# Strips of a Toeplitz convolution: half-strips on two queues, two channel pairs of prefetch, and a fourth strip

## Chip, cores, metric

The kernel runs on one core of a Trainium2 chip (trn2). The metric is the device time of one execution in microseconds (us). Each kernel was run four times, the kernel before up to seven times beside it. The kernel before takes 2420 us.

## The reference

Two stages follow one another. The first is a causal long convolution along the sequence, per channel; the second is a token mixer with two large dense matrices.

```python
B, S, D = 8, 5696, 128
def _attn_ref(x, h):                      # x: B,S,D   h: S,D
    L = 2 * S
    Yf = np.fft.rfft(x, n=L, axis=1) * np.fft.rfft(h, n=L, axis=0)[None]
    return np.fft.irfft(Yf, n=L, axis=1)[:, :S, :].astype(np.float32)
def _moe_ref(x, w_theta, w_tok_r, w_tok_i, w_ch):
    theta = x @ w_theta
    y = einsum('ts,bsd->btd', w_tok_r, x * cos(theta)) + einsum('ts,bsd->btd', w_tok_i, x * sin(theta))
    u = x + y
    return u + np.maximum(u @ w_ch, 0.0)
```

Only the convolution matters here; it is done in bf16 by matrix products instead of an FFT.

## The kernel before

The sequence is cut into 45 blocks of 128. For each channel `d` and each lag `k` of 0 to 44, TensorE multiplies a 128x128 Toeplitz block of `h` with the blocks of `x` that lag so far behind. A Toeplitz block is a window of a "strip": partition `p` of a strip holds the padded filter row of the channel, shifted by `p` elements, so the load is a DMA whose source rows start 2 bytes apart. The lags are cut into strips. Two of them are loaded into 64 partitions only, with 64 extra columns; the other 64 partitions are the same data shifted by 64 and are copied on the chip. The third is loaded in full.

```python
LAGS = ((0, 2 * KX, 64), (2 * KX, 31, 64), (31, NT, 0))      # KX = 8, NT = 45
# pool of strips: bufs=4 for each of strip0, strip1, strip2, stripq
def conv_strips(d):
    for n_, (k0, k1, halo) in enumerate(LAGS):
        w = (k1 - k0) * P
        strip = csb.tile([P, w + halo], BF16, ...)
        if halo == 0:                       # all 128 partitions
            nc.sync.dma_start(strip, AP(h_pad, [[1, P], [1, w]]));  continue
        lower = (d + n_) % 2 == 0
        own, other, c0, c1 = (lower half, upper half, 0, 64) if lower else (upper, lower, 64, 0)
        nc.sync.dma_start(strip[own, :], AP(h_pad, [[1, 64], [1, w + 64]]))
        if n_ == 0: nc.vector.tensor_copy(strip[other, c0:c0 + w], strip[own, c1:c1 + w])
        else:       nc.scalar.activation(strip[other, c0:c0 + w], strip[own, c1:c1 + w], AF.Copy)
    q_ = stripq;  nc.vector.tensor_add(q_, s0_[:, c0:c0 + w], s0_[:, c0 + P:c0 + P + w])
def conv_prepare(d):                        # a pair of channels
    xp = ...;  nc.scalar.activation(xp, xy[:, :, :, d:d + 2], AF.Copy)
    strips = [conv_strips(d + e) for e in range(2)]
    vd = ...;  nc.vector.tensor_sub(vd, xp even blocks, xp odd blocks)

nxt = conv_prepare(0)
for d in range(0, D, 2):
    xp, vd, strips = nxt
    nxt = conv_prepare(d + 2)               # one pair ahead, as written
    for e in range(2):
        # ... 8 products into c_ps, 17 of strip0 and stripq, 29 of the other strips into r_ps
    nc.scalar.activation(c_sb, c_ps, AF.Copy)
    nc.vector.tensor_tensor(xy even, r_ps even, c_sb, op=add)        # and odd: subtract
```

The code is shortened; `...` stands for what was left out. `stripq` holds sums of neighbouring blocks of `strip0`, and `vd` differences of neighbouring blocks of `x`; they spare products and stay as they are.

In the timelines shown below, ScalarE runs its instructions in the order in which they were built into the program. "Order" below always means that of the built program.

Of the kernel before, what the change touches and what calls it, by code (L numbers as in the profile page):

```python
# [11 lines left out]
BF16 = mybir.dt.bfloat16  # L12
add = mybir.AluOpType.add
mult = mybir.AluOpType.mult
AF = mybir.ActivationFunctionType
# [6 lines left out]
def kernel(  # L22
# [10 lines left out]
    nc = tc.nc  # L33
    B, S, D = x.shape
    assert D == 128
    P = 128
    NT = (S + P - 1) // P
    Sp = NT * P
    S_last = S - (NT - 1) * P
    HW = Sp + P  # L40
# [11 lines left out]
    h_pad = h_pad_h.ap()  # L52
# [25 lines left out]
    with tc.tile_pool(name="s0", bufs=1) as s0, \  # L78
# [27 lines left out]
        for tj in range(NT):  # L106
            q_cnt = P if tj < NT - 1 else S_last
            tmp = xl.tile([P, B, D], F32, tag="xt")
            if q_cnt < P:
# [3 lines left out]
                                      ap=[[D, q_cnt], [S * D, B], [1, D]]))  # L113
# [15 lines left out]
    KX = 8  # L129
    NJ2 = (NT + 1) // 2  # L130
    assert NT == 2 * NJ2 - 1
    LAGS = ((0, 2 * KX, 64), (2 * KX, 31, 64), (31, NT, 0))
    with tc.tile_pool(name="conv_strip", bufs=4) as csb, \
         tc.tile_pool(name="conv_x", bufs=3) as cxb, \
         tc.tile_pool(name="conv_psum", bufs=2, space=bass.MemoryType.PSUM) as cps:

        def conv_strips(d):

            out_ = []
            for n_, (k0, k1, halo) in enumerate(LAGS):  # L140
                w = (k1 - k0) * P
                strip = csb.tile([P, w + halo], BF16, tag=f"strip{n_}", name=f"strip{n_}")
                src = h_pad.offset + d * HW + P * k0
                if halo == 0:
                    nc.sync.dma_start(strip, bass.AP(tensor=h_pad.tensor, offset=src,
                                                     ap=[[1, P], [1, w]]))
                    out_.append((strip, 0, k0))
                    continue
                lower = (d + n_) % 2 == 0
                own, other, c0, c1 = ((slice(0, 64), slice(64, P), 0, 64) if lower else  # L150
                                      (slice(64, P), slice(0, 64), 64, 0))
                nc.sync.dma_start(strip[own, :],
                                  bass.AP(tensor=h_pad.tensor, offset=src,
                                          ap=[[1, 64], [1, w + 64]]))
                if n_ == 0:
                    nc.vector.tensor_copy(strip[other, c0:c0 + w], strip[own, c1:c1 + w])  # L156
                else:
                    nc.scalar.activation(strip[other, c0:c0 + w], strip[own, c1:c1 + w], AF.Copy)  # L158
                out_.append((strip, c0, k0))
            s0_, c0, _ = out_[0]  # L160
            w = (2 * KX - 1) * P
            q_ = csb.tile([P, w], BF16, tag="stripq", name="stripq")
            nc.vector.tensor_add(q_, s0_[:, c0:c0 + w], s0_[:, c0 + P:c0 + P + w])  # L163
            return out_, q_

        def conv_prepare(d):

            if d >= D:
                return None
            xp = cxb.tile([P, NJ2, 2, B, 2], BF16, tag="xp", name="xp")  # L170
            nc.scalar.activation(xp.rearrange("q j p b e -> q (j p b) e"),  # L171
                                 xy[:, :, :, d:d + 2].rearrange("q t b e -> q (t b) e"), AF.Copy)
            strips = [conv_strips(d + e) for e in range(2)]
            vd = cxb.tile([P, NJ2, B, 2], BF16, tag="vd", name="vd")
            nc.vector.tensor_sub(vd.rearrange("q j b e -> q j (b e)"),
                                 xp[:, :, 0, :, :].rearrange("q j b e -> q j (b e)"),
                                 xp[:, :, 1, :, :].rearrange("q j b e -> q j (b e)"))
            return xp, vd, strips

        nxt = conv_prepare(0)  # L180
        for d in range(0, D, 2):
            xp, vd, strips = nxt
            nxt = conv_prepare(d + 2)
            r_ps = cps.tile([P, 2, 512], F32, tag="rps", name="r_ps")
            c_ps = cps.tile([P, 2, 256], F32, tag="cps", name="c_ps")
            for e in range(2):
                (s0_, s1_, s2_), q_ = strips[e]
                r = r_ps[:, e, :NT * B]
                rj = r_ps[:, e, :2 * NJ2 * B].rearrange("q (j p b) -> q j p b", p=2, b=B)
                c_ = c_ps[:, e, :NJ2 * B]  # L190
                xt = xp.rearrange("q j p b e -> q (j p b) e")
                strip, c0, _ = s0_
                for k in range(KX):
                    n = NJ2 - k
                    b_ = strip[:, c0 + 2 * k * P:c0 + (2 * k + 1) * P]
                    nc.tensor.matmul(c_[:, B * k:], b_, vd[:, :n, :, e],  # L196
                                     start=(k == 0), stop=(k == KX - 1))
                    nc.tensor.matmul(rj[:, k:NJ2 - 1, 1, :], q_[:, 2 * k * P:(2 * k + 1) * P],  # L198
                                     xp[:, :n - 1, 0, :, e], start=(k == 0), stop=False)
                    nc.tensor.matmul(rj[:, k:, 0, :],  # L200
                                     q_[:, (2 * k - 1) * P:2 * k * P] if k else b_,
                                     xp[:, :n, 1, :, e], start=False, stop=False)
                nc.tensor.matmul(rj[:, KX:, 0, :], strip[:, c0 + (2 * KX - 1) * P:c0 + 2 * KX * P],
                                 xp[:, :NJ2 - KX, 1, :, e], start=False, stop=False)
                for strip, c0, k0 in (s1_, s2_):
                    k1 = LAGS[1][1] if strip is s1_[0] else NT
                    for k in range(k0, k1):
                        c = c0 + (k - k0) * P
                        nc.tensor.matmul(r[:, B * k:B * NT], strip[:, c:c + P],  # L209
                                         xt[:, :B * (NT - k), e], start=False, stop=(k == NT - 1))  # L210
            rv = r_ps[:, :, :2 * NJ2 * B].rearrange("q e (j p b) -> q p j b e", p=2, b=B)
            c_sb = cxb.tile([P, NJ2, B, 2], F32, tag="csb", name="c_sb")
            nc.scalar.activation(c_sb.rearrange("q j b e -> q (j b) e"),
                                 c_ps[:, :, :NJ2 * B].rearrange("q e n -> q n e"), AF.Copy)
            cv = c_sb
            yv = xy[:, :, :, d:d + 2].rearrange("q (j p) b e -> q p j b e", p=2)
            nc.vector.tensor_tensor(yv[:, 0], rv[:, 0], cv, op=add)  # L217
            nc.vector.tensor_tensor(yv[:, 1, :NJ2 - 1], rv[:, 1, :NJ2 - 1], cv[:, :NJ2 - 1],
                                    op=ALU.subtract)
# [147 lines left out]
    with tc.tile_pool(name="bpool", bufs=1, reuse_waits="tile") as bp, \  # L367
# [174 lines left out]
        def prepare(i, at_once=True):  # L542
            if i >= len(stretches):
                return None
            k, p, tt, j0, s0, nj = stretches[i]
            if s0 == 0:
                loads(k + 1)
            if tt is None:
                a1, a2 = (w_t(wb, s0, nj, ng=2) for wb in loaded[k])
                return a1, a2, w_sum(a1, a2, add, nj, m=64)  # L550
            w11, w22, w12, w21 = loaded[k]
            a = {}

            def step(n):

                if n == 0:
                    a[M3] = w_t(w11, s0, nj)
                elif n == 1:
                    a[M4] = w_t(w22, s0, nj)
                elif n == 2:  # L560
                    a["12"] = w_t(w12, s0, nj)
                    a[M5] = w_sum(a[M3], a["12"], add, nj)
                elif n == 3:
                    a["21"] = w_t(w21, s0, nj)
                    a[M2] = w_sum(a["21"], a[M4], add, nj)
                elif n == 4:
                    a[M1] = w_sum(a[M3], a[M4], add, nj)
                elif n == 5:
                    a[M7] = w_sum(a["12"], a[M4], ALU.subtract, nj)
                else:  # L570
                    a[M6] = w_sum(a["21"], a[M3], ALU.subtract, nj)
            if at_once:
                for n in range(7):
                    step(n)
                return a
            return a, step

        nxt, second, st = None, None, {}
        loads(0)
        for i, (k, p, tt, j0, s0, nj) in enumerate(stretches):  # L580
            first_of_pair = j0 + s0 == 0
            end_of_pair = j0 + s0 + nj == NJ
            if first_of_pair and tt == 0:
                start_pass(p)
                if p == 0:
# [4 lines left out]
                    nxt = prepare(0)  # L590
# [7 lines left out]
            a, nxt = nxt, prepare(i + 1, not woven)  # L598
            if woven:
                nxt, step = nxt  # L600
            if tt is None:
# [6 lines left out]
                for j in range(nj):  # L608
                    jj = j0 + s0 + j
                    for r in range(2):  # L610
                        b = [x[:, r, :] for x in bts[jj]]
# [7 lines left out]
                if end_of_pair:  # L619
# [5 lines left out]
                    for h in range(2):  # L625
                        c, c0 = cs[h]
# [22 lines left out]
            for n, q in enumerate(ORDER):  # L649
# [16 lines left out]
                if n == 1 and spread and (p == 1 or not end_of_pair):  # L666
                    where_bg["tags"] = ("c2", "c3") if j0 + s0 == TJ else ("red", "mag")
                    _, first, second = spread.pop(0)
# [45 lines left out]
```

## Time and profile before

Four runs took 2416.59 to 2425.41 us, median 2419.45 us. The convolution runs from about 111 us (first product) to 660 us (last), 64 pairs at about 8.6 us. What comes after it, about 1765 us, is untouched by the change.

| 200 to 500 us of the kernel before | value |
|---|---|
| TensorE busy | 251 of 300 us |
| VectorE, ScalarE busy | 171 us, 176 us |
| share of time in which the 16 DMA engines are busy | 1.04 (packets overlap a little) |
| DMA rate | 235 GB/s |

The table of windows, kernel before. The columns are the stretch and its length, then the busy time of TensorE (PE), its weight loads (PEld), VectorE (DVE), ScalarE (ACT) and GpSimd (POOL), the granted clock, the DMA share and GB/s:

```profile
core 0: us, PE busy (x) PEld busy (x) DVE busy (x) ACT busy (x) POOL busy (x), PEclk, DMA share, GB/s
200.00:500.00 300.00, 251.13 (x3830) 237.40 (x3827) 170.88 (x247) 175.72 (x142) 0.00 (x0) 0.99 1.04 235
```

The view of waits in that stretch, longest first, and below it that of the sync queue (SPq), kernel before. "DVE strip <- DMA strip<-h_pad: 113.9, 68" says that VectorE, about to copy a strip, waited 113.9 us in 68 waits for a strip to land:

```profile
DVE strip L156 <- DMA strip<-h_pad: 113.9, 68, 4.0
ACT strip L158 <- DMA strip<-h_pad: 66.2, 39, 3.0
ACT xp L171 <- PE r_ps L209: 55.1, 35, 2.3
```

```profile
SPq L152 <- DMA strip<-h_pad: 149.2, 137, 2.8
SPq L145 <- DMA strip<-h_pad: 41.1, 70, 1.3
```

The DMA issues of the strips (count, size of one, median us from issue to landing) and the chain of waits by line between 300 and 320 us, kernel before:

```profile
strip<-h_pad SPq DMA_DIRECT2D x128, 448.0 KB, 11.5
strip<-h_pad SPq DMA_DIRECT2D x128, 264.0 KB, 11.4
...
strip<-h_pad SPq DMA_DIRECT2D x128, 248.0 KB, 10.7
```

```profile
by line: DMA strip<-h_pad 104.3%; issue 9.3%; ACT strip L158 7.7%; ACT xp L171 4.9%; PE r_ps L209 3.8%; ACT c_sb L213 1.5%; ACTq L158 0.1%; ACTq L171 0.1%
```

These lines say that the copies wait for strips, that the queue itself waits for older strips to land, and that the DMA engines never rest. One transfer lands 11 us after its issue although there are six in every 8.6 us. The chain is the DMA. (A piece of the chain counts in full where it began before the stretch, so the shares can add up to more than 100%.)

### The profile page before, as it was taken

Reading aid. Unit: us, or ns where it says so; the run is one execution under the profiler, and the core shown is the slowest. Engines: PE = TensorE matmul, PEld = TensorE weight load, DVE = VectorE, ACT = ScalarE, POOL = GpSimd, SP = SyncE. Lnnn points to the kernel's source line nnn. Section 1 sums busy time; section 2 is a strip of 40 time slices with the busy share of each in tenths; the row PEclk is TensorE's granted clock in tenths of the full one; section 3 lists DMA queues with packets and bytes.
Section 4 is the critical chain, followed back from the end, with each engine's and each line's share of the span. In section 5 each row is a group of like instructions: output and inputs, shape, how many; then the busy total and the mean of one; then the engine's idle time right before and its main releaser. Section 6 shows DMA issues by size and latency. Waiting matters only on the chain.

```text
span 2426.1 us, 42014 instructions
## 1 busy us (share of the span) xinstructions
PE 2167.8 (89%) x15665; PEld 1237.5 (51%) x15838; DVE 1684.1 (69%) x3062; ACT 728.1 (30%) x861; POOL 796.7 (33%) x1474
## 2 busy tenths in 40 slices
PE   4578888888865799999999999979999999999997
PEld 1177787877742344444444444424444444444443
DVE  3355555555577788888688777787776777777774
ACT  3555655565583333333233000001110111111111
POOL 0000000000011344544445655335445445444540
PEclk8599999999997899999999999989999999999998
DMA  9999999999899789988889998878779779778872
GB/s 242 242 214 225 237 240 234 237 238 235 207 285 305 150 159 168 164 159 165 137 158 167 158 159 139 228 153 144 135 136 158 133 130 160 137 134 149 143 133 60
DMA packets 443532, 433.97 MB, mean 179 GB/s; under 512 B 66496, under 2 KB 370624, under 8 KB 443200
## 3 DMA queue, kind: packets, MB, share of 16 engines
q1 hardware_dynamic: 217488, 288.86, 45.8%
q0 software_dynamic: 222816, 131.33, 41.6%
q10 hardware_dynamic: 3024, 11.08, 1.2%
q8 instruction: 125, 2.05, 0.4%
q14 instruction: 79, 0.65, 0.1%
HBM read 477.58 MB, written 84.75 MB: 232 GB/s over the span
## 4 chain that ended last, share of the span: by engine, by line
PE 61%; DMA 24%; DVE 8%; issue 2%; ACT 2%; POOL 2%; SPq 1%; DVEq 0%; ACTq 0%; another core or an unknown queue 0%; POOLq 0%
PE m L653 50%; DMA strip<-h_pad 15%; PE r_ps L209 2%; DVE c L660 2%; DMA wb<-in_moe_w_tok_i_dram 2%; DMA tmp<-in_x_dram 2%; POOL wb L381 1%; DMA b<-zi_hbm 1%; DMA wb<-in_moe_w_tok_r_dram 1%; DMA h_bf<-in_h_dram 1%; DVE stripq L163 1%; PE r_ps L198 1%; PE utp L467 1%; PE v L474 1%; DVE wt L390 1%
## 5 line engine op out<-in xcount | busy, mean ns | idle before, releaser
L381 POOL DMA_DIRECT2D wb<-in_moe_w_tok_i_dram x720 | 389.1, 548 | 797.5 <-DVE wt L390 711.9
L381 POOL DMA_DIRECT2D wb<-in_moe_w_tok_r_dram x720 | 387.9, 548 | 777.5 <-DVE xy L217 656.6
L653 PE MATMUL m<-b,wt 128*128 128x512 bf16 x1892 | 452.7, 383 | 18.7 <-DVE b L322 6.8
L390 DVE STREAM_TRANSPOSE wt<-wb 128x384 f32<-128x384 f32 (+2 forms) x720 | 359.4, 523 | 118.3 <-PE m L653 72.4
L653 PEld LDWEIGHTS <-wt 128*128 128x128 bf16 x1936 | 190.4, 99 | 250.8 <-issue 23.2
L660 DVE TENSOR_TENSOR c<-c,m 128x512 f32<-128x512 f32 x440 | 283.3, 669 | 0.0
L158 ACT ACTIVATE strip<-strip 64x1920 bf16<-64x1920 bf16 x128 | 230.7, 1802 | 133.4 <-DMA strip<-h_pad 129.7
L469 ACT ACTIVATE uts<-utp 128x512 bf16<-128x512 bf16 (+1 forms) x90 | 53.3, 592 | 616.3 <-PE utp L467 616.3
L156 DVE COPY strip<-strip 64x2048 bf16<-64x2048 bf16 x128 | 88.2, 689 | 214.3 <-DMA strip<-h_pad 214.1
L209 PE MATMUL r_ps<-xp,strip 128*128 128x232 bf16 (+28 forms) x3712 | 228.9, 216 | 1.4 <-ACT strip L158 1.1
L198 PE MATMUL r_ps<-xp,stripq 128*128 128x176 bf16 (+7 forms) x1024 | 153.9, 229 | 78.4 <-DVE stripq L163 77.7
L209 PEld LDWEIGHTS <-strip 128*128 128x128 bf16 x3712 | 220.4, 96 | 5.2 <-ACT strip L158 2.1
L163 DVE TENSOR_TENSOR stripq<-strip 128x1920 bf16<-128x1920 bf16 x128 | 147.5, 1153 | 2.2
L198 PEld LDWEIGHTS <-stripq 128*128 128x128 bf16 x1024 | 98.8, 97 | 96.9 <-DVE stripq L163 96.2
L200 PE MATMUL r_ps<-xp,stripq 128*128 128x176 bf16 (+6 forms) x896 | 130.1, 229 | 0.0
L464 ACT ACTIVATE ub<-c 128x512 bf16<-128x512 f32 (+1 forms) x90 | 56.4, 628 | 225.7 <-DVE c L660 225.5
L196 PE MATMUL c_ps<-vd,strip 128*128 128x184 bf16 (+7 forms) x1024 | 93.3, 232 | 19.8 <-DVE strip L156 18.9
L240 ACT ACTIVATE yT<-tpz 128x512 bf16<-128x512 bf16 x68 | 39.8, 597 | 195.6 <-PE tpz L236 154.2
L118 PE MATMUL rps<-tmpbf,R_bf 128*128 128x512 bf16 x88 | 45.2, 617 | 51.1 <-DVE tmpbf L115 49.7
L200 PEld LDWEIGHTS <-stripq 128*128 128x128 bf16 x896 | 86.5, 96 | 0.0
L171 ACT ACTIVATE xp<-xy 128x736 bf16<-128x736 bf16 x64 | 55.4, 869 | 96.2 <-PE r_ps L209 96.1
L196 PEld LDWEIGHTS <-strip 128*128 128x128 bf16 x1024 | 71.8, 96 | 24.1 <-DVE strip L156 23.4
(2776 smaller groups left out, 3486.1 us busy)
## 6 DMA issues: line engine op xcount, KB each, us to landing
strip<-h_pad SPq DMA_DIRECT2D x128, 448.0 KB, 11.5
strip<-h_pad SPq DMA_DIRECT2D x128, 264.0 KB, 11.4
wb<-in_moe_w_tok_r_dram POOLq DMA_DIRECT2D x352, 96.0 KB, 4.5
wb<-in_moe_w_tok_i_dram POOLq DMA_DIRECT2D x352, 96.0 KB, 4.7
strip<-h_pad SPq DMA_DIRECT2D x128, 248.0 KB, 10.7
wb<-in_moe_w_tok_r_dram POOLq DMA_DIRECT2D x352, 80.0 KB, 4.5
wb<-in_moe_w_tok_i_dram POOLq DMA_DIRECT2D x352, 80.0 KB, 3.8
tmp<-in_x_dram SPq DMA_DIRECT2D x44, 512.0 KB, 6.4
```

The source lines that it names most:

```text
L156: nc.vector.tensor_copy(strip[other, c0:c0 + w], strip[own, c1:c1 + w])
L158: nc.scalar.activation(strip[other, c0:c0 + w], strip[own, c1:c1 + w], AF.Copy)
L163: nc.vector.tensor_add(q_, s0_[:, c0:c0 + w], s0_[:, c0 + P:c0 + P + w])
L196: nc.tensor.matmul(c_[:, B * k:], b_, vd[:, :n, :, e], start=(k == 0), stop=(k == KX - 1))
L198: nc.tensor.matmul(rj[:, k:NJ2 - 1, 1, :], q_[:, 2 * k * P:(2 * k + 1) * P], xp[:, :n - 1, 0, :, e], start=(k == 0), stop=False)
L200: nc.tensor.matmul(rj[:, k:, 0, :], q_[:, (2 * k - 1) * P:2 * k * P] if k else b_, xp[:, :n, 1, :, e], start=False, stop=False)
L209: nc.tensor.matmul(r[:, B * k:B * NT], strip[:, c:c + P], xt[:, :B * (NT - k), e], start=False, stop=(k == NT - 1))
L381: nc.gpsimd.dma_start(wb[32 * i:32 * i + 32, :ng, :nj * 64], bass.AP(tensor=a.tensor, offset=a.offset + row0 * S + p * H + i * QR + j0 * 6 ...
L390: nc.vector.transpose(wt.rearrange("p j t r -> p (j t r)").bitcast(F32).rearrange("p (j g t) -> p g j t", j=TJ, g=4)[:, :ng, :nj], wb[:, : ...
L464: nc.scalar.activation(ub[:m].rearrange("p b d -> p (b d)"), c[:m], AF.Copy)
L653: nc.tensor.matmul(ms[q], a[q][:, j, :, r], bts[jj][q][:, r, :], start=(jj == 0 and r == 0), stop=(jj == NJ - 1 and r == 1 and q not in left))
L660: nc.vector.tensor_tensor(c, z, ms[q], op=op)
```

## The change

It means to take the loads apart from the copies, to fetch two pairs ahead, to let a lower and an upper half arrive side by side on two queues, and to fetch fewer bytes: the third strip is cut in two, and the first part of it (7 lags) is fetched as a half, with VectorE making the other half. (In the diff `...` and the comment in `conv_fill` stand for code left out.) The number of buffers of each strip goes from 4 to 6 with it.

```diff
-    LAGS = ((0, 2 * KX, 64), (2 * KX, 31, 64), (31, NT, 0))
-    with tc.tile_pool(name="conv_strip", bufs=4) as csb, \
+    LAGS = ((0, 2 * KX, "v"), (2 * KX, 31, "s"), (31, 38, "v"), (38, NT, ""))
+    with tc.tile_pool(name="conv_strip", bufs=6) as csb, \
...
+        def conv_load(d):
...
+                    if not by:
+                        (nc.sync if e else nc.scalar).dma_start(
+                            strip, bass.AP(tensor=h_pad.tensor, offset=src, ap=[[1, P], [1, w]]))
...
+                    lower = (e + n_) % 2 == 0
...
+                    (nc.sync if lower else nc.scalar).dma_start(
+                        strip[own, :], bass.AP(tensor=h_pad.tensor, offset=src,
+                                               ap=[[1, 64], [1, w + 64]]))
...
+        def conv_fill(d, pair):
+            # xp (ScalarE); per channel: copies "v" on VectorE, "s" on ScalarE, stripq; vd
...
-        nxt = conv_prepare(0)
+        ahead = [conv_load(0), conv_load(2)]
+        nxt = conv_fill(0, ahead.pop(0))
         for d in range(0, D, 2):
-            xp, vd, strips = nxt
-            nxt = conv_prepare(d + 2)
+            xp, vd, pair, qs = nxt
+            ahead.append(conv_load(d + 4))
+            nxt = conv_fill(d + 2, ahead.pop(0))
```

A channel fetches 264 + 248 + 120 + 224 = 856 KB instead of 264 + 248 + 448 = 960 KB.

More of the change, by code (lines that the diff above doesn't have):

```diff
@@ L131 @@
     assert NT == 2 * NJ2 - 1
-    LAGS = ((0, 2 * KX, 64), (2 * KX, 31, 64), (31, NT, 0))
-    with tc.tile_pool(name="conv_strip", bufs=4) as csb, \
+    LAGS = ((0, 2 * KX, "v"), (2 * KX, 31, "s"), (31, 38, "v"), (38, NT, ""))
+    with tc.tile_pool(name="conv_strip", bufs=6) as csb, \
          tc.tile_pool(name="conv_x", bufs=3) as cxb, \
          tc.tile_pool(name="conv_psum", bufs=2, space=bass.MemoryType.PSUM) as cps:
-        def conv_strips(d):
-            out_ = []
-            for n_, (k0, k1, halo) in enumerate(LAGS):
-                w = (k1 - k0) * P
-                strip = csb.tile([P, w + halo], BF16, tag=f"strip{n_}", name=f"strip{n_}")
-                src = h_pad.offset + d * HW + P * k0
-                if halo == 0:
-                    nc.sync.dma_start(strip, bass.AP(tensor=h_pad.tensor, offset=src,
-                                                     ap=[[1, P], [1, w]]))
-                    out_.append((strip, 0, k0))
-                    continue
-                lower = (d + n_) % 2 == 0
-                own, other, c0, c1 = ((slice(0, 64), slice(64, P), 0, 64) if lower else
-                                      (slice(64, P), slice(0, 64), 64, 0))
-                nc.sync.dma_start(strip[own, :],
-                                  bass.AP(tensor=h_pad.tensor, offset=src,
-                                          ap=[[1, 64], [1, w + 64]]))
-                if n_ == 0:
-                    nc.vector.tensor_copy(strip[other, c0:c0 + w], strip[own, c1:c1 + w])
-                else:
-                    nc.scalar.activation(strip[other, c0:c0 + w], strip[own, c1:c1 + w], AF.Copy)
-                out_.append((strip, c0, k0))
-            s0_, c0, _ = out_[0]
-            w = (2 * KX - 1) * P
-            q_ = csb.tile([P, w], BF16, tag="stripq", name="stripq")
-            nc.vector.tensor_add(q_, s0_[:, c0:c0 + w], s0_[:, c0 + P:c0 + P + w])
-            return out_, q_
-        def conv_prepare(d):
@@ new lines, in conv_load @@
+        def conv_load(d):
+            if d >= D:
+                return None
+            pair = []
+            for e in range(2):
+                out_ = []
+                for n_, (k0, k1, by) in enumerate(LAGS):
+                    w = (k1 - k0) * P
+                    strip = csb.tile([P, w + (64 if by else 0)], BF16, tag=f"strip{n_}", name=f"strip{n_}")
+                    src = h_pad.offset + (d + e) * HW + P * k0
+                    if not by:
+                        (nc.sync if e else nc.scalar).dma_start(
+                            strip, bass.AP(tensor=h_pad.tensor, offset=src, ap=[[1, P], [1, w]]))
+                        out_.append((strip, 0, None, None))
+                        continue
+                    lower = (e + n_) % 2 == 0
+                    own, other, c0, c1 = ((slice(0, 64), slice(64, P), 0, 64) if lower else
+                                          (slice(64, P), slice(0, 64), 64, 0))
+                    (nc.sync if lower else nc.scalar).dma_start(
+                        strip[own, :], bass.AP(tensor=h_pad.tensor, offset=src,
+                                               ap=[[1, 64], [1, w + 64]]))
+                    out_.append((strip, c0, strip[other, c0:c0 + w], strip[own, c1:c1 + w]))
+                pair.append(out_)
+            return pair
@@ L172, in conv_prepare @@
                                  xy[:, :, :, d:d + 2].rearrange("q t b e -> q (t b) e"), AF.Copy)
-            strips = [conv_strips(d + e) for e in range(2)]
-            vd = cxb.tile([P, NJ2, B, 2], BF16, tag="vd", name="vd")
-            nc.vector.tensor_sub(vd.rearrange("q j b e -> q j (b e)"),
-                                 xp[:, :, 0, :, :].rearrange("q j b e -> q j (b e)"),
-                                 xp[:, :, 1, :, :].rearrange("q j b e -> q j (b e)"))
-            return xp, vd, strips
-        nxt = conv_prepare(0)
+            qs = []
+            for e in range(2):
+                for (strip, c0, to, from_), (k0, k1, by) in zip(pair[e], LAGS):
+                    if by == "v":
+                        nc.vector.tensor_copy(to, from_)
+                    elif by == "s":
+                        nc.scalar.activation(to, from_, AF.Copy)
+                    if k0 == 0:
+                        w = (2 * KX - 1) * P
+                        q_ = csb.tile([P, w], BF16, tag="stripq", name="stripq", bufs=4)
+                        nc.vector.tensor_add(q_, strip[:, c0:c0 + w], strip[:, c0 + P:c0 + P + w])
+                        qs.append(q_)
+                if e == 0:
+                    vd = cxb.tile([P, NJ2, B, 2], BF16, tag="vd", name="vd")
+                    nc.vector.tensor_sub(vd.rearrange("q j b e -> q j (b e)"),
+                                         xp[:, :, 0, :, :].rearrange("q j b e -> q j (b e)"),
+                                         xp[:, :, 1, :, :].rearrange("q j b e -> q j (b e)"))
+            return xp, vd, pair, qs
+        ahead = [conv_load(0), conv_load(2)]
+        nxt = conv_fill(0, ahead.pop(0))
         for d in range(0, D, 2):
-            xp, vd, strips = nxt
-            nxt = conv_prepare(d + 2)
+            xp, vd, pair, qs = nxt
+            ahead.append(conv_load(d + 4))
+            nxt = conv_fill(d + 2, ahead.pop(0))
             r_ps = cps.tile([P, 2, 512], F32, tag="rps", name="r_ps")
@@ L186 @@
             for e in range(2):
-                (s0_, s1_, s2_), q_ = strips[e]
+                q_ = qs[e]
                 r = r_ps[:, e, :NT * B]
@@ L191 @@
                 xt = xp.rearrange("q j p b e -> q (j p b) e")
-                strip, c0, _ = s0_
+                strip, c0 = pair[e][0][:2]
                 for k in range(KX):
@@ L204 @@
                                  xp[:, :NJ2 - KX, 1, :, e], start=False, stop=False)
-                for strip, c0, k0 in (s1_, s2_):
-                    k1 = LAGS[1][1] if strip is s1_[0] else NT
+                for (strip, c0, _, _), (k0, k1, _) in zip(pair[e][1:], LAGS[1:]):
                     for k in range(k0, k1):
```

## The prediction

> **What bounds it now.** The change touches only the convolution, which the timeline shows from 111 us to 661 us: 64 channel pairs, 8.5 to 8.6 us each. It is bound by the DMA engines. In the stretch from 200 to 600 us, the table of windows gives a DMA share of 1.03 at 235 GB/s, while TensorE is busy 333 of 400 us, VectorE 228, ScalarE 233. The view of waits has the first copy (VectorE) waiting 156 us and ScalarE's copy 88 us for strips; the sync queue itself waits 255 us for earlier strips to land, so about eight transfers are always outstanding. The critical chain there is almost all "DMA strip<-h_pad".
>
> **What the change removes.** A channel now fetches 264 + 248 + 448 = 960 KB. Splitting the last strip (7 lags fetched as a half of 120 KB, 7 in full as 224 KB) makes it 856 KB: 10.8% fewer bytes, 1.75 MB instead of 1.97 MB a pair.
>
> **What it adds.** VectorE: a copy of 64x896, by the trace's 689 ns for 64x2048 an estimated 0.30 us a channel; VectorE then has about 5.5 us of work a pair. ScalarE: four DMA issues a pair; at the 0.33 to 0.45 us that one takes on the sync queue, about 1.7 us. ScalarE has 233/47 = 5.0 us a pair, so it comes to 6.7 us, in order, behind buffer and landing waits: close to the new period. More and shorter rows (1792 and 1920 bytes instead of 3584): small.
>
> **What it moves.** Two pairs of prefetch and lower/upper halves on two queues. I give that nothing by itself. The Trainium skill, "DMA: Bandwidth & Descriptors", section "Issuing engines are not separate DMA queues", says that all queues run on the same 16 engines; "SBUF — State Buffer", section "Can I just issue two DMAs to hit both halves?", measured only +6%. The trace agrees: its packet records in steady state show 14 to 15 bytes/ns an engine for lower half, upper half and full strips alike, whatever the mix in flight (225 GB/s with few full strips in flight, 240 with many). So the limit is bytes, not port halves, and deeper prefetch cannot help where the DMA engines never idle.
>
> **Sum.** 1.753 MB at 231 to 235 GB/s is 7.46 to 7.6 us a pair; TensorE's own work is 333/47 = 7.1 us a pair, a floor. With ScalarE at 6.7 us and in-order waits I allow 0.15 us of loss: about 7.65 us, 490 us for the stage instead of 546 us. All of that is on the critical path; later stages don't change. Predicted: 2364 us, 80% range 2335 to 2402. Chances: faster by over 2% 0.62, within 2% 0.35, slower 0.03.
>
> **What would show it.** Right: the stage shrinks to about 490 us with DMA share still about 1.0 at 225 to 245 GB/s, TensorE about 93% busy, strip bytes down 10.8%, waits for strips smaller but still there. If two queues do raise the rate, GB/s goes over 245, the DMA share falls below 0.95 and TensorE becomes the limit (stage about 465 us, total 2336). If ScalarE is the new limit, its queue never rests, the DMA share falls while GB/s stays at or below 225, and TensorE waits for ScalarE's copies.
>
> **What would make it wrong.** ScalarE's in-order DMA issues blocking on landings or buffers and delaying its copies, eating most of the gain (total 2390 to 2410); half-strips being slower than full ones once they are 74% of the bytes (now 53%); or the byte limit being really a limit of outstanding transfers, which more depth or two queues would lift.

## More of the kernel before

ScalarE's timeline (start, duration, queue or engine, line, instruction; in brackets the idle time before it), kernel before:

```profile
401.34 0.96 ACT L171 ACTIVATE xp<-xy 128x736 bf16<-128x736 bf16 x1 [1.38 <-PE r_ps L209]
402.32 1.80 ACT L158 ACTIVATE strip<-strip 64x1920 bf16<-64x1920 bf16 x1
405.77 1.80 ACT L158 ACTIVATE strip<-strip 64x1920 bf16<-64x1920 bf16 x1 [1.65 <-DMA strip<-h_pad]
407.60 0.48 ACT L213 ACTIVATE c_sb<-c_ps 128x368 f32<-128x368 f32 x1
```

L171 is `xp`, L158 the copy of strip1 (one for each channel of a pair), L213 `c_sb`, which needs TensorE's products into `c_ps`.

## The result and the profile after

Four runs took 2345.04 to 2381.43 us, median 2358.43 us; the longest counts as slow. The ratio is 0.9726, 95% interval 0.9676 to 0.9777: faster. Here and below, a ratio is the mean time of one kernel's runs over that of the kernel before in the same rounds, so it is not quite the ratio of the medians. Executions over 1.5% slower than the fastest of the same kernel are left out of the means. The experiments below ran on other chips, on which the kernel before had medians of 2428 to 2433 us; ratios are therefore compared, not times.

The same windows, waits, first three of eight kinds of issues, and chain, kernel after:

```profile
200.00:500.00 300.00, 284.32 (x4478) 276.62 (x4476) 237.16 (x374) 206.22 (x167) 0.00 (x0) 1.00 1.05 245
```

```profile
ACT xp L168 <- DVE strip L174: 58.2, 27, 3.3
DVE strip L174 <- DMA strip<-h_pad: 55.5, 77, 2.0
ACT xp L168 <- PE r_ps L219: 21.4, 10, 2.4
ACT xp L168 <- DMA strip<-h_pad: 13.1, 5, 3.2
```

```profile
strip<-h_pad SPq DMA_DIRECT2D x64, 264.0 KB, 7.2
strip<-h_pad ACTq DMA_DIRECT2D x64, 264.0 KB, 7.2
strip<-h_pad ACTq DMA_DIRECT2D x64, 248.0 KB, 6.7
...
```

```profile
by line: DMA strip<-h_pad 34.2%; PE r_ps L219 16.2%; DVE stripq L180 11.6%; PE c_ps L207 10.2%; DVE strip L174 7.4%; PE r_ps L211 7.1%; PE r_ps L209 6.5%; DVE xy L227 2.3%; DVE xy L228 2.2%; DVE vd L184 1.8%; issue 1.3%; PE r_ps L214 0.5%; 
```

TensorE is now busy 284 of 300 us, while the DMA share is still 1.05. VectorE's wait for strips fell from 114 to 56 us, ScalarE's copies no longer appear among the waits at all, and the DMA's part of the chain went from all of it to a third, shared with TensorE and VectorE. ScalarE's longest waits are now those before `xp` (58 us ended by VectorE's copies, 21 us by TensorE, 13 us by landings); its queue also holds DMA issues, which wait there. The last product of the convolution starts at 588 us instead of 660 us. The stretch after it takes as long as before (1763 against 1765 us), so the whole gain is in the convolution.

Two details of ScalarE. First its timeline in the middle of the stage, then at its start, kernel after (ACTq is ScalarE's own queue of DMA issues):

```profile
401.73 0.45 ACTq L156 DMA_DIRECT2D strip<-h_pad  x1
402.23 0.90 ACT L168 ACTIVATE xp<-xy 128x736 bf16<-128x736 bf16 x1 [1.91 <-PE r_ps L219]
403.15 1.80 ACT L176 ACTIVATE strip<-strip 64x1920 bf16<-64x1920 bf16 x1
403.95 0.45 ACTq L156 DMA_DIRECT2D strip<-h_pad  x1
404.44 0.77 ACTq L149 DMA_DIRECT2D strip<-h_pad  x1
404.98 1.80 ACT L176 ACTIVATE strip<-strip 64x1920 bf16<-64x1920 bf16 x1
406.81 0.48 ACT L223 ACTIVATE c_sb<-c_ps 128x368 f32<-128x368 f32 x1
408.11 0.45 ACTq L156 DMA_DIRECT2D strip<-h_pad  x1
```

```profile
107.61 0.60 ACTq L149 DMA_DIRECT2D strip<-h_pad  x1
...
116.51 3.41 ACTq L156 DMA_DIRECT2D strip<-h_pad  x2
119.97 0.83 ACT L168 ACTIVATE xp<-xy 128x736 bf16<-128x736 bf16 x1 [12.27 <-DMA strip<-h_pad]
120.83 1.80 ACT L176 ACTIVATE strip<-strip 64x1920 bf16<-64x1920 bf16 x1
```

At the start, ScalarE issues the loads of the second pair ahead of the copies of the first, blocks on landings, and makes the first `xp` only at 120 us; the first product comes at 121 us instead of 111 us. This loses 10 us once. And in the built program, ScalarE makes both strip copies of the *next* pair before `c_sb` of the pair in work. In the kernel before, it made the copies of a pair immediately before `c_sb` of that same pair. The lists of the built programs show it by tile numbers:

```
before, ScalarE                        after, ScalarE
strip1_8859<-strip1_8859               strip1_4630<-strip1_4630
strip1_8869<-strip1_8869               strip1_4638<-strip1_4638
c_sb_9126<-c_ps_9017                   c_sb_4912<-c_ps_4803
TensorE: r_ps_9016<-xp_8854,strip1_8869
                                       TensorE: c_ps_4803<-vd_4651,strip0_4484
```

In the kernel before, the pair whose products go to 9016 and 9017 reads strip1_8869, copied just ahead. In the kernel after, the pair of 4803 reads strips numbered about 4484; 4630 and 4638 belong to the next pair. The program text asks for copies one pair ahead in both; the framework that builds the kernel may move instructions.

### The profile page after: what moved, and what is told of

Its sections match the earlier page's. It is cut to its first block, busy times and chain, and to the rows that moved or that the text cites. A ratio compares the mean times of both kernels' runs of the same rounds, so it can differ in the third digit from the quotient of the medians.

```text
span 2352.5 us, 42205 instructions
## 1 busy us (share of the span) xinstructions
PE 2151.8 (91%) x15665; PEld 1238.1 (53%) x15838; DVE 1738.3 (74%) x3190; ACT 728.6 (31%) x861; POOL 795.3 (34%) x1474
## 4 chain that ended last, share of the span: by engine, by line
PE 63%; DMA 24%; DVE 8%; issue 2%; ACT 1%; POOL 1%; SPq 1%; DVEq 0%; ACTq 0%; POOLq 0%
PE m L663 54%; DMA strip<-h_pad 15%; DVE c L670 2%; DMA tmp<-in_x_dram 2%; DMA wb<-in_moe_w_tok_r_dram 1%; PE r_ps L219 1%; DMA b<-zi_hbm 1%; DMA wb<-in_moe_w_tok_i_dram 1%; DMA h_bf<-in_h_dram 1%; PE v L484 1%; PE utp L477 1%; DVE wt L400 1%; POOL wb L391 1%; PE m L625 1%; PE m L627 1%
## 5 line engine op out<-in xcount | busy, mean ns | idle before, releaser
L176 ACT ACTIVATE strip<-strip 64x1920 bf16<-64x1920 bf16 x128 | 230.7, 1802 | 3.1
L209 PE MATMUL r_ps<-xp,stripq 128*128 128x176 bf16 (+7 forms) x1024 | 203.2, 226 | 31.0 <-DVE xy L228 15.6
L219 PEld LDWEIGHTS <-strip 128*128 128x128 bf16 x3712 | 220.1, 96 | 1.6
L174 DVE COPY strip<-strip 64x2048 bf16<-64x2048 bf16 (+1 forms) x256 | 137.7, 539 | 105.2 <-DMA strip<-h_pad 99.2
L207 PE MATMUL c_ps<-vd,strip 128*128 128x184 bf16 (+7 forms) x1024 | 192.1, 232 | 9.9 <-DVE vd L184 9.4
L211 PE MATMUL r_ps<-xp,stripq 128*128 128x176 bf16 (+6 forms) x896 | 180.5, 228 | 0.0
L207 PEld LDWEIGHTS <-strip 128*128 128x128 bf16 x1024 | 97.3, 96 | 17.6 <-issue 17.0
L168 ACT ACTIVATE xp<-xy 128x736 bf16<-128x736 bf16 x64 | 56.3, 879 | 151.2 <-DVE strip L174 79.1
```

Of the source, the lines that this page charges most:

```text
L174: nc.vector.tensor_copy(to, from_)
L176: nc.scalar.activation(to, from_, AF.Copy)
L207: nc.tensor.matmul(c_[:, B * k:], b_, vd[:, :n, :, e], start=(k == 0), stop=(k == KX - 1))
L209: nc.tensor.matmul(rj[:, k:NJ2 - 1, 1, :], q_[:, 2 * k * P:(2 * k + 1) * P], xp[:, :n - 1, 0, :, e], start=(k == 0), stop=False)
L211: nc.tensor.matmul(rj[:, k:, 0, :], q_[:, (2 * k - 1) * P:2 * k * P] if k else b_, xp[:, :n, 1, :, e], start=False, stop=False)
L219: nc.tensor.matmul(r[:, B * k:B * NT], strip[:, c:c + P], xt[:, :B * (NT - k), e], start=False, stop=(k == NT - 1))
```

## The experiments

Twelve runs were made (e11 is the kernel after once more). All gave a correct result. Pair time is taken from the first to the last start of the products with `stripq` in the profiled run, divided by 63.5; share and rate are those of 200 to 500 us. "Pairs ahead" counts the loads.

| run | queues | pairs ahead | KB a channel | order | ratio (95%) | us a pair | DMA share, GB/s |
|---|---|---|---|---|---|---|---|
| before | 1 | 1 | 960 | free | 1 | 8.60 | 1.04, 235 |
| after | 2 | 2 | 856 | free | 0.9726 (0.968 to 0.978) | 7.33 | 1.05, 245 |
| e1_one_queue | 1 | 2 | 856 | free | 1.0215 (1.018 to 1.025) | 9.38 | 0.69, 188 |
| e2_bytes_only | 1 | 1 | 856 | free | 1.0195 (1.016 to 1.023) | 9.33 | 0.70, 189 |
| e3_no_byte_cut | 2 | 2 | 960 | free | 0.9957 (0.991 to 1.000) | 8.45 | 1.01, 236 |
| e4_one_ahead | 2 | 1 | 856 | free | 0.9826 (0.978 to 0.988) | 8.06 | 1.03, 223 |
| e5_one_queue_pinned | 1 | 2 | 856 | pinned | 0.9720 (0.966 to 0.978) | 7.65 | 1.03, 233 |
| e6_after_pinned | 2 | 2 | 856 | pinned | 0.9726 (0.967 to 0.978) | 7.74 | 1.04, 228 |
| e7_before_pinned | 1 | 1 | 960 | pinned | 1.0036 (0.998 to 1.009) | 8.70 | 1.03, 232 |
| e8_bytes_only_pinned | 1 | 1 | 856 | pinned | 0.9796 (0.974 to 0.985) | 7.68 | 1.02, 232 |
| e9_all_half | 1 | 2 | 752 | pinned | 0.9557 (0.951 to 0.961) | 6.93 | 0.94, 231 |
| e10_all_half_pool | 1 | 2 | 752 | pinned | 0.9594 (0.955 to 0.964) | 6.94 | 0.93, 228 |
| e11_after_again | 2 | 2 | 856 | free | 0.9736 (0.968 to 0.980) | 7.52 | 1.03, 235 |
| e12_one_queue_act_pinned | 1 | 2 | 856 | ScalarE pinned | 0.9748 (0.971 to 0.979) | 7.70 | 1.04, 234 |

The theories at the start: mine, that bytes are the gain and that two queues give nothing. Rival A: one queue to each half of the partitions raises the DMA rate. Rival B: depth of prefetch is the gain.

### One queue

```diff
-                        (nc.sync if e else nc.scalar).dma_start(
+                        nc.sync.dma_start(
-                    (nc.sync if lower else nc.scalar).dma_start(
+                    nc.sync.dma_start(
```

> The changed kernel with all strip loads issued on the sync queue; bytes, depth and copies as in the change. My theory (the gain is the bytes; two queues give nothing by themselves): within 10 us of the changed kernel's 2354 us, convolution at 245 GB/s as before, perhaps a few us faster because ScalarE no longer issues loads and its queue does not block on landings (the first pair could start earlier than the 121 us of the changed kernel). Rival A (two queues, one to each half of the partitions, raise the rate of the DMA engines): the rate falls back to about 235 GB/s, a pair takes about 7.5 us instead of 7.3, the total is 10 to 20 us longer.

It took 2480 us, 50 us more than the kernel before on its chip. That refutes what I expected, but it isn't what rival A expected either: the DMA share fell to 0.69. The DMA engines were idle a third of the time, so their rate was not the bound. The windows, waits and ScalarE's timeline of this run:

```profile
200.00:500.00 300.00, 220.94 (x3425) 209.42 (x3423) 183.99 (x286) 159.39 (x128) 0.00 (x0) 1.00 0.69 188
```

```profile
DVE xy L227 <- PE r_ps L219: 108.9, 32, 3.8
PEld L219 <- ACT strip L176: 89.8, 64, 1.8
ACT c_sb L223 <- issue: 80.7, 32, 2.8
PE r_ps L219 <- ACT strip L176: 79.1, 64, 1.6
```

```profile
402.07 0.87 ACT L168 ACTIVATE xp<-xy 128x736 bf16<-128x736 bf16 x1 [1.88 <-PE r_ps L219]
402.97 1.80 ACT L176 ACTIVATE strip<-strip 64x1920 bf16<-64x1920 bf16 x1
407.27 0.48 ACT L223 ACTIVATE c_sb<-c_ps 128x368 f32<-128x368 f32 x1 [2.50 <-issue]
407.77 1.80 ACT L176 ACTIVATE strip<-strip 64x1920 bf16<-64x1920 bf16 x1
```

`c_sb` (L223) now stands between the two strip copies (L176) and sits idle 2.5 us before it runs. TensorE waits for a strip copy 64 times in the stretch (two for each of its 32 pairs, as 300 us at 9.38 us a pair make 32), 79 us in all. The instruction list of the built program says which pair is which:

```
e1_one_queue, ScalarE                       e12_one_queue_act_pinned, ScalarE
xp_6084                                     strip1_5782<-strip1_5782
strip1_5638<-strip1_5638                    strip1_5790<-strip1_5790
c_sb_6064<-c_ps_5955                        c_sb_6064<-c_ps_5955
strip1_5646<-strip1_5646                    xp_6084
xp_6228                                     strip1_5926<-strip1_5926
```

TensorE's products into `c_ps_5955` read `strip0_5636` and `strip0_5644`: the pair in work has the strips 5638 and 5646. So ScalarE copies the second strip1 of a pair only after `c_sb` of the *same* pair, and `c_sb` waits for TensorE's products of the second channel. TensorE then needs that copy at once. The copy for the first channel is late too: it stands behind an `xp` of a later pair, which sits idle 1.88 us for TensorE's last products of the pair before. Each pair waits twice for a copy of 1.80 us that could have been made long ago, and no load two pairs ahead helps. Moving the loads to another queue had changed the order in which the copies were built into ScalarE's stream.

### Fewer bytes, nothing else

```diff
-    LAGS = ((0, 2 * KX, 64), (2 * KX, 31, 64), (31, NT, 0))
+    LAGS = ((0, 2 * KX, 64), (2 * KX, 31, 64), (31, 38, 64), (38, NT, 0))
-                if n_ == 0:
+                if n_ != 1:
                     nc.vector.tensor_copy(strip[other, c0:c0 + w], strip[own, c1:c1 + w])
```

(in the kernel before; one queue, one pair ahead)

> The kernel before with the last strip split in two, nothing else: one queue, one pair ahead, old order. My theory (bytes): 856 KB a channel at 235 GB/s, so 7.45 us a pair, stage about 70 us shorter less what in-order waits cost; total 2360 to 2375 us. Rival B (prefetch depth and loads issued apart from the fills bring the gain): less than 25 us of the 65 us, total over 2395 us.

It took 2476 us, 2% slower than before, with 11% fewer bytes. The instruction list shows the same order as in the one-queue run: `c_sb` between the two strip copies of its own pair. Both misses therefore show the same thing, and they say nothing yet of bytes or queues.

### Two queues and two pairs ahead, without the byte cut

```diff
-    LAGS = ((0, 2 * KX, "v"), (2 * KX, 31, "s"), (31, 38, "v"), (38, NT, ""))
+    LAGS = ((0, 2 * KX, "v"), (2 * KX, 31, "s"), (31, NT, ""))
```

> The changed kernel with the old three strips: two queues and two pairs ahead, but 960 KB a channel. My theory: the DMA engines stay full at 235 to 245 GB/s, so 8.0 to 8.4 us a pair and at most 30 us gained; at exactly the old rate nothing is gained but the start is lost (total 2390 to 2425 us). Rival A or B: most of the 65 us are gained, total under 2375 us.

Ratio 0.9957. Its order on ScalarE is that of the kernel after (copies one pair ahead), and it has the queues and the depth, but the DMA engines are full (1.01 at 236 GB/s): 1.97 MB a pair at that rate is 8.33 us, and 8.45 were measured. Without the byte cut next to nothing is gained. (TensorE's granted clock in this stretch was 0.94, against 0.99 before; with TensorE busy 256 of 300 us and the DMA engines full, nothing shows that this set the time.)

### One pair ahead

```diff
-        ahead = [conv_load(0), conv_load(2)]
+        ahead = [conv_load(0)]
-            ahead.append(conv_load(d + 4))
+            ahead.append(conv_load(d + 2))
```

> The changed kernel with loads one pair ahead instead of two. My theory: the DMA engines can no longer run ahead while ScalarE fills, so something is lost, but less than half: total 2355 to 2385 us. Rival B (depth is the gain): back over 2395 us.

Ratio 0.9826 (2387 us, just over the range expected) against 0.9726 and 0.9736 of the two measurements of the kernel after: the second pair of prefetch is probably worth about 1 point of the 2.7, although the DMA share was 1.03 in this run too. The intervals touch or overlap a little. ScalarE's built order is the good one here too. The rate in the profile is 223 GB/s instead of 235 to 245, but that profile is of the slowest of the four runs (2395 us; the fastest took 2373 us), and a two-queue kernel with two pairs ahead, below, shows 228. A DMA share of 1 does therefore not tell the rate; why packets take longer in some runs is left open.

### Order pinned: four kernels

The framework offers a call that pins an instruction behind the one written before it on its engine. It is meant to fix the order only. It was put around every product, copy and sum of the convolution.

```diff
+    in_order = tc.keep_in_program_order
-            nc.scalar.activation(xp..., AF.Copy)
+            in_order(nc.scalar.activation(xp..., AF.Copy))
...                       # and so for each nc.vector, nc.scalar and nc.tensor call of the loop, not for the loads
```

One queue, pinned:

> All strip loads on the sync queue again, but the convolution's instructions on TensorE, VectorE and ScalarE are pinned to the order in which the program writes them. In the first one-queue run ScalarE's order was c_sb of a pair, then the second strip copy of that same pair, so a pair waited for itself. Theory C (the two queues helped because they made the compiler put every pair's copies one pair ahead; the DMA engines don't care): 2340 to 2362 us, no slower than the changed kernel, convolution at 7.1 to 7.4 us a pair. Rival A (two queues raise the rate of the DMA engines): order in place, but the rate stays at 235 GB/s or below, 7.5 us a pair or more, total over 2368 us.

The kernel after, pinned:

> Control: the changed kernel with the same pinning. Its copies already ran one pair ahead, so both theories say within 10 us of 2354 us.

The kernel before, pinned:

> The kernel before with the same pinning: its copies then come before c_sb of the pair in work instead of after it. My theory (at 960 KB a channel the DMA engines are the bound, order is hidden under them): 2410 to 2430 us, as before. If order alone were the gain: under 2375 us.

Fewer bytes only, pinned:

> The kernel before with four strips, as in the run that lost 50 us, now pinned. Theory C (the fewer bytes are the gain, and need the copies one pair ahead): the gain comes, total 2350 to 2385 us with one queue and one pair of prefetch. Rival A/B (the queues or the depth are needed on the chip): over 2400 us.

The windows of the one-queue kernel and of the kernel after, both pinned, on the same chip:

```profile
200.00:500.00 300.00, 268.01 (x4276) 264.18 (x4274) 228.58 (x355) 193.56 (x160) 0.00 (x0) 1.00 1.03 233
```

```profile
200.00:500.00 300.00, 262.31 (x4170) 258.71 (x4168) 222.97 (x348) 189.57 (x155) 0.00 (x0) 0.99 1.04 228
```

With the order held, one queue reaches 0.9720 and two queues 0.9726, at 233 and 228 GB/s. The times expected were a little low (2366 us measured for both), but this chip is slower by half a per cent, and the ratios are those of the kernel after. By itself the one-queue run did not come out as theory C said: 7.65 us a pair at 233 GB/s is what rival A had forecast for the stage. What decides is the control: two queues in the same order, on the same chip, take 7.74 us at 228 GB/s. Rival A falls: the queues do nothing measurable on the chip. The order alone gains nothing either (before, pinned: 1.0036; its 2443 us are over the range expected), because at 960 KB the DMA engines bind (share 1.03 at 232 GB/s). (The expectation misstates the old order: there the copies stood right before `c_sb` of their own pair, as the lists above show.) The byte cut with the order held, with one queue and one pair ahead, gives 0.9796, three quarters of the gain; unpinned, the same edit had lost 2%. The two pinned one-queue kernels with one and two pairs ahead hardly differ in the stage (7.68 and 7.65 us a pair, 232 and 233 GB/s).

### Only ScalarE pinned

The one-queue kernel with only the ScalarE calls wrapped as above, those of VectorE and TensorE left free.

> The first one-queue run (ratio 1.0215) with only ScalarE's five instructions a pair pinned to program order; TensorE and VectorE are left to the compiler. If ScalarE's order alone (c_sb of a pair before the second strip copy of the same pair) made the loss: ratio 0.970 to 0.985. If the order on VectorE or TensorE, or the one queue, has a part in it: 0.99 or more.

Ratio 0.9748. Pinning ScalarE's instructions turns a loss of about 2% into a gain of 2.5%. ScalarE's timeline, to be held against that of the free one-queue run above:

```profile
402.49 0.48 ACT L226 ACTIVATE c_sb<-c_ps 128x368 f32<-128x368 f32 x1
402.86 0.99 ACT L171 ACTIVATE xp<-xy 128x736 bf16<-128x736 bf16 x1
404.32 1.80 ACT L179 ACTIVATE strip<-strip 64x1920 bf16<-64x1920 bf16 x1 [0.47 <-DMA strip<-h_pad]
407.95 1.80 ACT L179 ACTIVATE strip<-strip 64x1920 bf16<-64x1920 bf16 x1 [1.83 <-DMA strip<-h_pad]
409.78 0.48 ACT L226 ACTIVATE c_sb<-c_ps 128x368 f32<-128x368 f32 x1
```

Both copies (L179) now stand ahead of `c_sb` (L226), which no longer waits. In the view of waits of this run, 200 to 500 us, TensorE's wait for ScalarE's copies has gone from 79.1 us to 2.4:

```profile
PE r_ps L212 <- ACT strip L179: 2.4, 7, 0.4
```

That the built order made the loss is with this shown. That it was ScalarE's part of it is shown less directly, because VectorE, though left free, was built in another order too. In e1_one_queue VectorE copies `strip2_5640`, `strip0_5644` and `strip2_5648` of the pair in work only after the sums of the pair before it, in this run it copies those of the next pair there. No run changes ScalarE's order alone. What points at ScalarE is the view of waits of e1_one_queue: TensorE was idle 79 of 300 us, its waits for ScalarE's copies add up to 79.1 us, and none for a copy of VectorE's is listed.

### All strips as halves

```diff
-    LAGS = (..., (31, 38, "v"), (38, NT, ""))        # in the pinned one-queue kernel
+    LAGS = (..., (31, 38, "v"), (38, NT, "v"))
```

> The pinned one-queue version with the fourth strip fetched as a half too: 752 KB a channel instead of 856, its second half copied by VectorE (128 copies of 0.39 us more). If the bytes still bound the convolution, 1.54 MB a pair at 233 GB/s is 6.6 us, under TensorE's own 7.1 us: DMA share falls to about 0.93, a pair takes 7.1 to 7.3 us instead of 7.6, ratio to before 0.955 to 0.968. If instead order alone or the issue of loads is the bound, the ratio stays at 0.972 or more.

```profile
200.00:500.00 300.00, 295.06 (x4715) 291.06 (x4713) 286.15 (x480) 211.59 (x177) 0.00 (x0) 1.00 0.94 231
```

Ratio 0.9557, 2325 us: better than both kernels. The DMA share falls below 1, TensorE is busy 295 of 300 us, and the pair time of 6.93 us (less than expected) is now TensorE's. VectorE is busy 286 us, so it is nearly full as well. This is the third size of the loads at about the same rate (232, 233 and 231 GB/s): 960, 856 and 752 KB gave 8.70, 7.65 and 6.93 us with the order pinned (the first with one pair ahead), until TensorE took over.

With the fourth copy on GpSimd:

```diff
-    LAGS = (..., (31, 38, "v"), (38, NT, "v"))
+    LAGS = (..., (31, 38, "v"), (38, NT, "p"))
+                    elif by == "p":
+                        nc.gpsimd.tensor_copy(to, from_)
```

> The same, but GpSimd, idle in the convolution, makes the copy of the fourth strip. If VectorE's 6.5 us a pair are no bound: same ratio as with VectorE, within 0.004; if VectorE had become the bound: lower by up to 0.008; if GpSimd's copy is over 3 us long or disturbs VectorE: higher.

The groups of instructions from 200 to 500 us by form, VectorE, kernel with GpSimd's copy (line, engine, operation, tiles, shapes, count; busy us and mean ns of one; idle time before):

```profile
L175 DVE COPY strip<-strip 64x2048 bf16<-64x2048 bf16 x88 | 73.7, 838 | 2.7
L175 DVE COPY strip<-strip 64x896 bf16<-64x896 bf16 x88 | 41.8, 475 | 2.8
L187 DVE TENSOR_TENSOR vd<-xp 128x368 bf16<-128x368 bf16 x44 | 24.3, 552 | 1.4
```

Ratio 0.9594; its interval overlaps that of the kernel with VectorE's copy, though each of its four runs (2329 to 2342 us) is slower than each of the other's (2323 to 2326 us) on the same chip. GpSimd's copy took 1.03 us against 0.39 us on VectorE, and VectorE was not relieved: its copies of 64x2048 took 838 ns instead of 688 ns, those of 64x896 475 ns instead of 388 ns, the sum `vd` (128x368) 552 ns instead of 350 ns, and it was busy 289 of 300 us as against 286 us. The Trainium skill, "SBUF — State Buffer", section "Who interferes with whom", says that VectorE's copies in some modes and its sums of two SBUF operands share ports with GpSimd; the longer times agree, though `stripq`, a sum of two SBUF operands as well, grew only from 1158 to 1214 ns. Whether VectorE is a second bound beside TensorE stays open, since this run didn't take load off it.

### The kernel after, once more

> The changed kernel once more, on the chip of these runs, to have its ratio and its DMA rate beside them: ratio 0.970 to 0.978 as first measured. If the 245 GB/s of its first profile was the two queues' doing, it shows again here while the one-queue run stays at 233; if it was the chip or the run, the rates of these kernels agree within 5 GB/s while each is bound by the DMA engines.

Ratio 0.9736 and 235 GB/s. The 245 GB/s of the first profile was not the doing of two queues; three profiles of two-queue kernels with these bytes and this depth show 245, 228 and 235 GB/s, the two of one-queue kernels 233 and 234. With 7% between profiles of such kernels, a small difference in rate between one and two queues can't be excluded, but there is none in the totals. With two pairs ahead, one queue does start earlier: the first product comes at 110 to 113 us instead of 116 to 121 us. Two queues with one pair ahead (e4) start at 112 us, which points at the second pair's loads in ScalarE's queue; one queue with one pair ahead, pinned (e7, e8), starts at 117 us, so the start has other causes too.

## Why the prediction was right or wrong

The predicted 2364 us met 2358 us, within the range. The forecast held, but one of its steps does not hold, and it missed the built order of the copies, on which the gain depends. Point by point:

- **Bound by DMA, bytes are the gain.** Right. With 960 KB nothing helps (e3_no_byte_cut, e7_before_pinned), and each step of bytes moves the time (e8_bytes_only_pinned, e9_all_half). The stage was predicted to last 490 us; it lasted 467 us in the first profile from its own first product to its last, 477 us with the 10 us by which it started later, with pair times of 7.33 and 7.52 us in two profiles instead of 7.65.
- **"I give that nothing by itself", of the two queues.** Right about the chip, wrong about the kernel. The Trainium skill, "DMA: Bandwidth & Descriptors", section "Issuing engines are not separate DMA queues", says that queues of several engines run on the same 16 DMA engines; these runs agree (0.9720 with one, 0.9726 with two). But taking the second queue away cost 4.9 points (1.0215), because the built order of the copies changed with it. The prediction never considered that an edit to loads can reorder copies. That the change happened to come with the good order was luck, and without it the number would not have held.
- **Deeper prefetch "cannot help where the DMA engines never idle".** Probably wrong, by about 1 point (e4_one_ahead, intervals touching or overlapping a little); with one queue and the order pinned it is 0.8 (e8 against e5, intervals overlapping, and e8 has 4 buffers instead of 6), though a pair takes the same time there. What does not hold is the reading of a DMA share of 1.03 as a rate that can't rise: shares of 1.03 to 1.05 went with 223 to 245 GB/s, and two profiles of the very same kernel show 235 and 245.
- **ScalarE's DMA issues, 1.7 us a pair, close to the new period.** They did no harm in the steady state: with the order pinned, one queue is no faster. They did at the start: 10 us. The prediction named such blocking as a risk, but not for the start alone.
- **TensorE's floor of 7.1 us a pair.** Too high: e9_all_half ran at 6.93 us, with TensorE busy 295 of 300 us. Busy time of 333 us over 47 pairs is thus no floor; which part of it was waiting is not shown.
- **The profile after.** TensorE about 93% busy (95% measured), DMA share about 1.0 at 225 to 245 GB/s (1.05 at 245), strip bytes down 10.8%: right.

## What to carry to other kernels

When an edit to loads changes the time, compare the built order of every engine's instructions before blaming the transfers: a copy for the pair in work that stands behind a wait for that same pair cancels any prefetch, and the sign is a low DMA share with TensorE waiting for a short copy at a fixed period. Pin the order first, then measure queues, depth and bytes one by one. If the DMA engines are full and the data is redundant, fetch half and copy the rest on an engine that has time; it worked here down to the point where TensorE became the bound.

## What the Trainium skill lacked or had wrong

- "DMA: Bandwidth & Descriptors", section "Rules for kernel authors", advises one 128-partition transfer instead of halves, and "SBUF — State Buffer", section on the DMA port swizzle, gives a transfer to 64 partitions about 60% of the rate of one to 128 (196 against 328 GB/s for 1 MiB). In this stream, where about eight transfers were in flight (an estimate: 11 us to land, six issued every 8.6 us) instead of one alone, half and full strips moved at the same rate: packet records of the kernel before, 200 to 600 us, show 3584 bytes in 251 ns (full) and 4224 bytes in 293 ns (half) on average, 14.3 and 14.4 bytes/ns for each DMA engine. Where the other half can be made on the chip, halves won, because they fetch fewer bytes (0.9557). So the figures for one transfer alone do not carry over to this stream; no run here tests them as such.
- "DMA: Bandwidth & Descriptors" has 341 GB/s for 1 MB to 128 partitions, issued from GpSimd; here, with loads of 120 to 448 KB issued from SyncE and ScalarE, the DMA engines of the DMA-bound kernels were busy all the time at 223 to 245 GB/s, with source rows starting 2 bytes apart. A later stage of the same run (661 to 800 us of the kernel before) moves 285 GB/s. No run here tells why.
- "Perfetto Trace Analysis" tells how to follow waits, but no page says that the queue of a load can change the order of other engines' instructions in the built program; it was worth 1.0215 against 0.9748, with one queue in both.
- "DMA: Bandwidth & Descriptors", section "Issuing engines are not separate DMA queues", calls the sequencer time of an issue usually small. No page gives a number for what issues on ScalarE's queue cost ScalarE's own work: here an issue took 0.45 us for a half-strip, and once, at the start of the stage, ScalarE stood idle for 12.27 us before the first `xp` while its queue waited for landings.
